# Loads, sums and transposes of the second and third batch put at other places, and the last output block in two parts, in a fused attention and mixer kernel

## The chip, the cores and the metric

The kernel runs on one core of a Trainium2 chip. The metric is the time of one execution on the device in microseconds, the median of several runs. A core has five engines that work side by side, each on its own list of instructions in order: TensorE (PE, matmuls; PEld is its weight load), VectorE (DVE), ScalarE (ACT), GpSimd (POOL) and SyncE (SP), which here only issues transfers. They meet through semaphores. Transfers (DMA) run beside them; those that SP issues show up as queue q1, those that GpSimd issues as q0, and ScalarE's as q10.

## The reference

Attention with normalized queries and keys, over 8 batches, 12 heads, 448 rows and 64 columns, and a mixer on the heads put side by side (448 x 768 for each batch):

```python
q_n = q / (norm(q) + 1e-6);  k_n = k / (norm(k) + 1e-6)
attn = softmax(q_n @ k_n.T / tau)
x = (attn @ v), heads side by side            # 448 x 768
u = x + (x.T @ U @ V).T                       # rank 32, over the rows
out = u + max(u @ w_ch1, 0) @ w_ch2           # 768 -> 3072 -> 768
```

## The kernel before

Heads are worked on in **pairs**, six in a batch, numbered 0 to 47 over all batches; `NP` is 6, so pairs 6 to 11 are batch 1 and 12 to 17 batch 2. Inputs come in **groups** of mostly two pairs: group 5 holds pairs 8 and 9, group 6 holds 10 and 11, group 7 holds 12 and 13, group 8 holds 14 and 15. A group's q, k and v are loaded by SP (`load`) into one of three staging buffers (`NST`), two transfers for q, four each for k and for v. Then the group is prepared (`Prep`): `square` of q and of k (mostly on GpSimd, L243), `reduce` to sums (VectorE, L248), `root` (ScalarE, L253 and L254), `invert` (VectorE, L260 and L262), `scale` (GpSimd, L268, four for a group), and `values`, the cast of v to bf16 (GpSimd, L276).

A pair's scaled q and k are transposed: up to pair 11 by eight matmuls on TensorE (L300) and a copy on VectorE (L305), from pair 12 on by a transposing transfer that SP issues (L315, name `T` in the schedule). Scores follow (L331, L324 and L343), their exponentials on ScalarE (L356, L353), the product with the values in two halves (L376, L383), each divided on VectorE (L394, then L395, which writes X). Both halves of a pair up to the tenth use the same PSUM bank. Then comes the low-rank part: `A` (L416, up to pair 10 with X as an operand), its copy on ScalarE (L422), X's transpose (L430) and `H` (L441) with its copy to u (L446). From pair 10 on these are done for two pairs at once, with X transposed by SP (L461), L469, L483 and the sums L488 into uE or uO, the two buffers of u. V, the rank-32 matrix, is needed for this in four copies, one on each 32 partitions: `load_copies` brings three more of them, `place_copies` casts them (L152 to L154).

The mixer of a batch is cut into small steps that fill TensorE between the attention steps of the next batch. `steps_m1` makes 24 blocks of six matmuls (L513, 448 columns) with a relu on ScalarE (L517) or VectorE (L519). `steps_m2` takes for each half of the 768 output columns three or four blocks of 128 rows, each 24 matmuls of 384 columns (L540) in four steps of six. Batch 0 adds u by three more matmuls (L550) and copies the block out on ScalarE (L554) or VectorE (L556); later batches add it on VectorE (L558). L564, L568 and L571 store the blocks. After the last pair, nothing but the last batch's mixer is left.

The order is written out by hand. Batch 0's attention has a list of words. From pair 6 on, a loop over `n` names a few places in each pair's turn (index 0, 1, ... of `order`), and between places puts as many mixer steps as `spread` gives. Preparations, loads and weight loads are hung on such places with `put(n, index, ...)`. A place fixes an instruction's turn in its engine's own list, and not a time: an engine that has nothing to wait for runs ahead. `Estimate` adds up rough costs for TensorE, ScalarE and VectorE while the program is written, and `act_first` picks from them the engine for a relu, or for batch 0's copy of a block:

```python
a = max(t["act"], t["pe"]) + act_us
d = max(t["dve"], t["pe"]) + dve_us
if a <= d: ...   # ScalarE, otherwise VectorE
```

The weights `w1_sb` and `w2_sb` are loaded on GpSimd's queue, w1 in four pieces and w2 in two halves of two pieces each: `load_w2(0, 0, 12)` and `load_w2(0, 12, 24)` for the first half of the columns. They are 32-bit in memory and arrive as bf16.

Of the kernel before, what the change touches and what calls it, by code (L numbers as in the profile page):

```python
# [9 lines left out]
FP = mybir.dt.float32  # L10
# [12 lines left out]
def kernel(  # L23
# [17 lines left out]
    nc = tc.nc  # L41

    B, H, S, D = q.shape
    C = H * D
    R = moe_U.shape[-1]
    F = moe_w_ch1.shape[-1]
    NP = H // 2
    CC = C // 128
    NC = F // 128
    HC = C // 2  # L50
# [3 lines left out]
    work = ctx.enter_context(tc.tile_pool(name="work", bufs=2))  # L54
# [30 lines left out]
    est = Estimate()  # L85
# [39 lines left out]
    V_raw = work.tile([128, S], FP, name="V_raw", tag="ut", bufs=2)  # L125
# [3 lines left out]
    w2_sb = const.tile([128, NC, C], BF, name="w2_sb")  # L129
# [29 lines left out]
    def load_copies():  # L159

        for r0 in (32, 64, 96):
            nc.gpsimd.dma_start(out=V_raw[r0:r0 + R, :], in_=moe_V)

    def place_copies():
        place_v(nc.gpsimd.tensor_copy, slice(0, 128))
# [5 lines left out]
    def load_w2(half, n0, n1):  # L171
        cols = slice(half * HC, (half + 1) * HC)
        nc.gpsimd.dma_start(
            out=w2_sb[:, n0:n1, cols],
            in_=moe_w_ch2[n0 * 128:n1 * 128, cols].rearrange("(n p) d -> p n d", p=128))


    groups = []
# [11 lines left out]
    def load(gi, what, *engs):  # L190
        b, p0, n = groups[gi]
        engs = list(engs) * 4
        h0, nh = 2 * p0, 2 * n
        s = gi % NST

        def src(x, hs, lo, hi, c):
            return x[b, hs, lo:hi, :].rearrange("h (p c) d -> p h (c d)", c=c)

        def dst(t, ps, hs, c):
            return t[ps, hs, 0:c, :].rearrange("p h c d -> p h (c d)")  # L200

        L, U2 = slice(0, 64), slice(64, 128)
        if what == "q":
            allh = slice(h0, h0 + nh)
            engs[0].dma_start(out=dst(qst[s], L, slice(0, nh), 4), in_=src(q, allh, 0, 256, 4))
            engs[1].dma_start(out=dst(qst[s], U2, slice(0, nh), 3), in_=src(q, allh, 256, 448, 3))
            return
        x, t = (k, kst[s]) if what == "k" else (v, vst[s])
        m = min(3, nh)
        ou, mi = slice(h0, h0 + nh, 3), slice(h0 + 1, h0 + m)  # L210
        engs[0].dma_start(out=dst(t, L, slice(0, nh, 3), 4), in_=src(x, ou, 0, 256, 4))
        engs[1].dma_start(out=dst(t, U2, slice(0, nh, 3), 3), in_=src(x, ou, 256, 448, 3))
        engs[2].dma_start(out=dst(t, L, slice(1, m), 3), in_=src(x, mi, 0, 192, 3))
        engs[3].dma_start(out=dst(t, U2, slice(1, m), 4), in_=src(x, mi, 192, 448, 4))
# [66 lines left out]
    def by_dma(n):  # L281

        return n >= 2 * NP
# [25 lines left out]
    def step_T(b, p):  # L309
        if not by_dma(b * NP + p):  # L310
            pe_T(b, p)
            evict_T(b, p)
            return
        gi, j = group_of[(b, p)]
        nc.sync.dma_start_transpose(  # L315
            out=new_qkT(b, p).rearrange("p a (c r) -> p (a c) r", r=128),
            in_=norm[gi][0][:, j, :, :, :, :].rearrange("p i c h d -> p (i c h d)"))
# [92 lines left out]
    def u_of(b):  # L410
        return uE if b % 2 == 0 else uO
# [82 lines left out]
    ut_of = {}  # L494
# [30 lines left out]
    def steps_m2(b):  # L525
        u = u_of(b)
        if b % 2 == 0:
            chunks = [(64 + 128 * c, 128 * c, c) for c in range(3)]
        else:
            chunks = [(384, 384, 3)] + [(128 * c, 128 * c, c) for c in range(3)]  # L530
        steps = []
        state = {}

        def part(half, ci, lo, hi):
            r0, u0, c = chunks[ci]
            if lo == 0:
                state["mp"] = psum.tile([128, HC], FP, name="mp", tag="ps_m", bufs=2)
            mp = state["mp"]
            for f in range(lo, hi):
                nc.tensor.matmul(out=mp, lhsT=relu[:, f, r0:r0 + 128],  # L540
                                 rhs=w2_sb[:, f, half * HC:(half + 1) * HC],
                                 start=(f == 0), stop=(b > 0 and f == NC - 1), skip_group_check=True)
            est.pe(0.97)
            if hi < NC:
                return
            o = work.tile([128, HC], FP, name="o_sb", tag="o_sb", bufs=3)
            if b == 0:
                for i in range(3):
                    cc = half * 3 + i
                    nc.tensor.matmul(out=mp[:, i * 128:(i + 1) * 128], lhsT=u[:, cc, u0:u0 + 128],  # L550
                                     rhs=ident, start=False, stop=(i == 2), skip_group_check=True)
                est.pe(0.17)
                if est.act_first(0.48, 0.55):
                    nc.scalar.copy(out=o, in_=mp)  # L554
                else:
                    nc.vector.tensor_copy(out=o, in_=mp)  # L556
            else:
                nc.vector.tensor_add(o.rearrange("p (k d) -> p k d", d=128),  # L558
                                     mp.rearrange("p (k d) -> p k d", d=128),
                                     ut_of[(b, half)][:, :, c, :])  # L560
                est.dve(0.55)
            cols = slice(half * HC, (half + 1) * HC)
            t4 = out[b, 0:256, cols].rearrange("(p c) d -> c p d", c=4)
            nc.sync.dma_start(out=t4[c], in_=o[0:64, :])  # L564
            if c < 3:
                t3 = out[b, 256:448, cols].rearrange("(p c) d -> c p d", c=3)
                other = nc.scalar if b == B - 1 and half == 1 else nc.sync
                other.dma_start(out=t3[c], in_=o[64:128, :])  # L568
            else:
                t4e = out[b - 1, 0:256, cols].rearrange("(p c) d -> c p d", c=4)  # L570
                nc.sync.dma_start(out=t4e[3], in_=o[64:128, :])  # L571

        for half in range(2):
            for ci in range(len(chunks)):
                for i in range(4):
                    steps.append(lambda half=half, ci=ci, i=i: part(half, ci, 6 * i, 6 * i + 6))
        return steps
# [8 lines left out]
    def f(n):  # L586
        for _ in range(n):
            fill.pop(0)()

    def load_all(gi):  # L590
        if gi < len(groups):
            for x in ("q", "k", "v"):
                load(gi, x, nc.sync)

    load(0, "k", nc.sync, nc.scalar)
    load(0, "q", nc.sync, nc.scalar)
# [10 lines left out]
    def T(n):  # L607
        step_T(*pairs[n])
# [124 lines left out]
    def put(n, at, fn):  # L733
        after.setdefault((n, at), []).append(fn)

    for gi in range(5, len(groups)):
        m, g = first_pair[gi], preps[gi]
        if m == NP + 2:
            at = [(NP, 1), (NP, 2), (NP + 1, 6), (NP, 5), (NP + 1, 0), (NP + 1, 1)]
            when = (NP + 1, 2)  # L740
        elif m == NP + 4:
            at = [(NP + 2, 0), (NP + 2, 1), (NP + 2, 6), (NP + 2, 4), (NP + 2, 6), (NP + 2, 7)]
            when = (NP + 3, 0)
        elif m == 2 * NP:
            at = [(m - 3, 6), (m - 3, 6), (m - 1, 0)] + [(m - 2, i) for i in (0, 1, 2)]
            when = (m - 2, 3)
        elif m == 2 * NP + 2:
            at = [(m - 2, i) for i in (0, 0, 5, 2, 3, 4)]
            when = (m - 2, 5)
        else:  # L750
            at = [(m - 3, 0), (m - 3, 0), (m - 3, 5)] + [(m - 2, i) for i in (0, 1, 2)]
            when = (m - 2, 3)

        put(*at[0], lambda g=g: g.square(0))
        put(*at[1], lambda g=g: g.square(1))
        put(*at[2], lambda g=g: g.values())
        put(*at[3], lambda g=g: g.reduce(0))
        put(*at[4], lambda g=g: g.reduce(1))
        put(*at[5], lambda g=g: g.root())
        put(*when, lambda g=g: (g.invert(), [g.scale(i, j, P_) for j in (0, 1) for i in (1, 0)]))  # L760
        if gi > 5 and m - 6 <= NP:
            put(*((NP, 3), (NP + 3, 0))[gi - 6], lambda gi=gi: load_all(gi))
        elif gi > 5:
            at = {2 * NP + 2: [(m - 4, 5), (m - 4, 6), (m - 3, 2)],
                  2 * NP + 4: [(m - 4, i) for i in (0, 2, 4)]}.get(m, [(m - 6, 4), (m - 5, 5), (m - 4, 3)])
            for x, w in zip("qkv", at):
                put(*w, lambda gi=gi, x=x: load(gi, x, nc.sync))
        if by_dma(m):
            put(m - 1, -1, lambda m=m: T(m))
            put(m - 1, 0, lambda m=m: T(m + 1))  # L770

    put(NP, 2, lambda: load_w1(2304, 3072))
    put(NP, 3, lambda: (load_w2(0, 0, 12), load_w2(0, 12, 24)))
    put(NP + 1, 2, lambda: (load_w2(1, 0, 12), load_w2(1, 12, 24)))
    put(NP + 3, 0, load_copies)
    put(NP + 5, 5, place_copies)

    def spread(n, order, nf, first=0):
# [14 lines left out]
    for n in range(NP, NPAIR + 1):  # L793
        b, p = pairs[n] if n < NPAIR else (B, 0)
# [116 lines left out]
```

## Time and profile before

| what | value |
|---|---|
| median of three runs | 581.62 us (581.51 to 582.03) |
| span of the profiled run | 580.3 us |
| TensorE busy | 568.6 us, 98% of the span |
| ScalarE, GpSimd, VectorE busy | 261.0, 215.1, 213.1 us |
| TensorE's clock granted | full speed throughout, but for the idle end |
| transfers | 74.52 MB, on average 128 GB/s |
| bytes on SP's queue and on GpSimd's | 63.03 MB and 10.18 MB |
| weight pieces on GpSimd's queue | 8, median 18.8 us from issue to landing |
| V's copies on GpSimd's queue | 56 KB each, median 17.4 us to landing |
| outputs on SP's queue | 96 KB each, median 2.2 us to landing |

A row of the stretches of busy time gives the stretch, its length, then each engine's busy time with the number of its instructions in brackets (TensorE, weight load, VectorE, ScalarE, GpSimd), the granted clock, the share of the sixteen DMA engines that was busy, and GB/s. A row of the waits reads: engine, tile and line that waited, what released it, microseconds in total, how many times, the longest. A row of the chain of waits gives start, length and what was done. A queue's row gives packets, MB and the time of its packets as a share of sixteen engines' time. Ends of matmuls are modelled, and a little later than the next matmul's start.

### The profile page before, as it was taken

The page shows a single profiled execution, that of the slowest core. Times are in us where ns is not written, and L with a number is a line of the kernel's source. Part 1 is how long each engine was busy: PE and PEld are TensorE (multiplying, and loading weights), DVE is VectorE, ACT ScalarE, POOL GpSimd, SP SyncE. Part 2 cuts the span into 40 slices and gives each one's busy share as a digit, 9 for nine tenths or more (in the row PEclk, how much of TensorE's full clock was granted, in tenths as well). Part 3 has the DMA queues.
Part 4 walks back from the last instruction along what each step waited for, and adds up shares of the span by engine and source line. Part 5 has one row for each costly group of instructions (what it writes and reads, how often), then busy time and mean ns, then how long its engine had stood idle before and what let it go on. Part 6 is the DMA issues. An engine that isn't in the chain of part 4 may idle for free.

```text
span 580.3 us, 12249 instructions
## 1 busy us (share of the span) xinstructions
PE 568.6 (98%) x5074; PEld 327.1 (56%) x5074; DVE 213.1 (37%) x461; ACT 261.0 (45%) x447; POOL 215.1 (37%) x205
## 2 busy tenths in 40 slices
PE   7999999999999999999999999999999999999997
PEld 6665565555565556555655555655555545655554
DVE  6874551433243334423324343432244332320011
ACT  5876544455333653446324455246443374214200
POOL 8754866515326236426055063253261420000000
PEclk9999999999999999999999999999999999999999
DMA  6999999767486375584465763783655640231022
GB/s 163 193 244 236 238 211 221 181 124 138 103 158 155 88 154 114 135 162 105 88 160 137 128 137 96 145 175 81 134 125 117 132 74 16 54 72 35 7 49 56
DMA packets 139673, 74.52 MB, mean 128 GB/s; under 512 B 86656, under 2 KB 139440, under 8 KB 139616
## 3 DMA queue, kind: packets, MB, share of 16 engines
q1 hardware_dynamic: 129344, 63.03, 50.0%
q0 software_dynamic: 9728, 10.18, 10.3%
q8 instruction: 40, 0.66, 0.4%
q10 hardware_dynamic: 544, 0.51, 0.3%
q14 instruction: 17, 0.14, 0.1%
HBM read 52.19 MB, written 11.01 MB: 109 GB/s over the span
## 4 chain that ended last, share of the span: by engine, by line
PE 87%; DMA 7%; DVE 2%; SPq 1%; ACT 1%; POOL 1%; issue 0%; DVEq 0%; POOLq 0%; ACTq 0%
PE mp L540 38%; PE mp L513 33%; DMA w_sb<-in_moe_w_ch_dram 5%; PE sc L331 5%; PE av L383 3%; PE up L383 2%; DMA kst<-in_k_dram 2%; PE av L343 1%; PE av L376 1%; PE up L376 1%; PE up L469 1%; DMA qst<-in_q_dram 1%; PE av L483 1%; DVE ss L248 1%; ACT E L356 0%
## 5 line engine op out<-in xcount | busy, mean ns | idle before, releaser
L540 PE MATMUL mp<-w_sb,relu 128*128 128x384 bf16 x1344 | 233.6, 327 | 0.8 <-DMA w_sb<-in_moe_w_ch_dram 0.8
L540 PEld LDWEIGHTS <-relu 128*128 128x128 bf16 x1344 | 125.2, 98 | 90.6 <-issue 14.0
L513 PEld LDWEIGHTS <-w_sb 128*128 128x128 bf16 x1128 | 105.0, 98 | 99.2 <-issue 9.3
L517 ACT ACTIVATE relu<-mp 128x448 bf16<-128x448 f32 x162 | 88.0, 543 | 128.4 <-PE mp L513 128.4
L356 ACT ACTIVATE E<-sc 128x896 bf16<-128x896 f32 x144 | 125.2, 923 | 23.6 <-PE sc L331 22.6
L268 POOL TENSOR_TENSOR qk<-kst,inv 128x512 bf16<-128x512 f32 x43 | 45.9, 1069 | 240.7 <-DVE inv L262 236.2
L513 PE MATMUL mp<-uO,w_sb 128*128 128x448 bf16 x576 | 114.3, 353 | 0.0
L513 PE MATMUL mp<-uE,w_sb 128*128 128x448 bf16 x552 | 112.9, 353 | 0.0
L558 DVE TENSOR_TENSOR o_sb<-mp,ut 128x384 f32<-128x384 f32 x50 | 27.8, 557 | 141.4 <-PE mp L540 140.1
L248 DVE TENSOR_REDUCE ss<-sq 128x16 f32<-128x1024 f32 (+1 forms) x50 | 57.8, 1165 | 1.0 <-ACT sq L240 1.0
L268 POOL TENSOR_TENSOR qk<-qst,inv 128x512 bf16<-128x512 f32 x44 | 47.3, 1077 | 1.6 <-PE up L441 1.6
L383 PEld LDWEIGHTS <-E 128*128 128x128 bf16 x1152 | 45.0, 97 | 0.0
L519 DVE TENSOR_SCALAR relu<-mp 128x448 bf16<-128x448 f32 x26 | 16.2, 625 | 78.0 <-PE mp L513 77.5
L331 PE MATMUL sc<-qkT 64*64 64x448 bf16 x576 | 42.4, 360 | 0.6 <-ACT E L356 0.3
L243 POOL TENSOR_TENSOR sq<-kst 128x1024 f32<-128x1024 f32 (+1 forms) x23 | 42.6, 1856 | 0.1
L243 POOL TENSOR_TENSOR sq<-qst 128x1024 f32<-128x1024 f32 x21 | 39.7, 1892 | 3.3 <-DMA qst<-in_q_dram 3.3
L353 ACT ACTIVATE E<-av 128x448 bf16<-128x448 f32 x17 | 9.2, 541 | 47.3 <-PE up L343 47.3
L276 POOL CAST v<-vst 128x1024 bf16<-128x1024 f32 (+1 forms) x25 | 25.0, 1003 | 9.9 <-DMA vst<-in_v_dram 7.7
L383 PE MATMUL av<-v,E 128*128 128x65 bf16 x624 | 28.0, 193 | 0.0
L473 ACT CAST A_sb<-up 128x128 bf16<-128x128 f32 x19 | 5.0, 263 | 47.6 <-PE up L469 47.6
L394 DVE RECIPROCAL rd<-av 128x4 f32<-128x4 f32 x52 | 9.3, 178 | 46.2 <-PE av L383 46.2
L376 PEld LDWEIGHTS <-E 128*128 128x128 bf16 x192 | 18.0, 98 | 14.6 <-issue 0.8
(98 smaller groups left out, 348.9 us busy)
## 6 DMA issues: line engine op xcount, KB each, us to landing
out_dram<-o_sb SPq DMA_DIRECT2D x109, 96.0 KB, 2.2
w_sb<-in_moe_w_ch_dram POOLq DMA_DIRECT2D x8, 1152.0 KB, 18.8
qst<-in_q_dram SPq DMA_DIRECT2D x23, 256.0 KB, 3.9
vst<-in_v_dram SPq DMA_DIRECT2D x46, 128.0 KB, 2.9
kst<-in_k_dram SPq DMA_DIRECT2D x44, 128.0 KB, 2.8
qst<-in_q_dram SPq DMA_DIRECT2D x23, 192.0 KB, 4.0
vst<-in_v_dram SPq DMA_DIRECT2D x46, 96.0 KB, 2.7
kst<-in_k_dram SPq DMA_DIRECT2D x44, 96.0 KB, 2.7
```

The lines of the kernel that those rows point to most:

```text
L243: nc.gpsimd.tensor_mul(sq[:, 0:self.nh * 4, :], self.flat(t), self.flat(t))
L248: nc.vector.reduce_sum(self.ss[:, j, 0:self.nh * 4], self.sq[j][:, 0:self.nh * 4, :], axis=AX.X)
L268: eng.tensor_mul(qks[self.gi % 2][:, j, i, :, :, :], t[:, 2 * j:2 * j + 2, :, :].rearrange("p h c d -> p c h d"), iv.unsqueeze(3).to_broad ...
L276: nc.gpsimd.tensor_copy(out=self.flat(v65[self.s])[:, :, 0:D], in_=self.flat(vst[self.s]))
L331: nc.tensor.matmul(out=sc[o:o + 64, h, 0:S], lhsT=t[r, 1, c * 128 + o:c * 128 + o + 64], rhs=t[r, 0, 0:S], start=True, stop=True)
L356: nc.scalar.activation(out=e[:, 2 * c:2 * c + 2, 0:S], in_=sc[:, :, 0:S], func=AF.Exp)
L376: nc.tensor.matmul(out=av[:, i, :, :], lhsT=last_of(b, p)[:, ic * 128:(ic + 1) * 128], rhs=vv[:, 2 * j:2 * j + 2, 3, :], start=(i == 0), s ...
L383: nc.tensor.matmul(out=av[:, i, h, :], lhsT=e[:, 2 * c + h, ic * 128:(ic + 1) * 128], rhs=vv[:, 2 * j + h, c, :], start=False, stop=(i == ...
L513: nc.tensor.matmul(out=mp, lhsT=w1_sb[:, cc, f * 128:(f + 1) * 128], rhs=u[:, cc, 0:S], start=(cc == 0), stop=(cc == CC - 1))
L517: nc.scalar.activation(out=relu[:, f, o:o + S], in_=mp, func=AF.Relu)
L540: nc.tensor.matmul(out=mp, lhsT=relu[:, f, r0:r0 + 128], rhs=w2_sb[:, f, half * HC:(half + 1) * HC], start=(f == 0), stop=(b > 0 and f == ...
L558: nc.vector.tensor_add(o.rearrange("p (k d) -> p k d", d=128), mp.rearrange("p (k d) -> p k d", d=128), ut_of[(b, half)][:, :, c, :])
```

## The change

It moves work of the second and third batch to other places, and splits the last output block:

- V's three copies are loaded on SP's queue instead of GpSimd's, and hung on pair 8 instead of pair 9.
- Group 5's sums, root and inverse take earlier places, in front of pair 7's turn. Group 7's second sum, root and inverse move ahead by one place each. Group 8's sums and root move back by one.
- Group 6's values are loaded at pair 8 instead of with q and k at pair 6, and cast at pair 10 instead of pair 8. Group 7's values are loaded at pair 10 instead of with q and k at pair 9. Group 8's q, k and v are asked for in pair 11's turn instead of pairs 10 and 11.
- The transposes of pair 12 are asked for at the end of pair 10's turn, in front of group 8's loads, and those of pair 13 just after.
- The very last block (24 matmuls of 384 columns) becomes one of 256 and one of 128 columns, each with its own add and its own stores, in steps of twelve matmuls. The number of steps stays four.
- The planner's cost for a step of L540 is worked out from its columns.

Its purpose is to have the sums and the weights ready when TensorE asks for them, and to leave less to do behind the last matmul.

```diff
     def load_copies():
         for r0 in (32, 64, 96):
-            nc.gpsimd.dma_start(out=V_raw[r0:r0 + R, :], in_=moe_V)
+            nc.sync.dma_start(out=V_raw[r0:r0 + R, :], in_=moe_V)
...
-        def part(half, ci, lo, hi):
+        def part(half, ci, lo, hi, c0=0, c1=HC):
...
-            mp = state["mp"]
+            mp = state["mp"][:, c0:c1]
             for f in range(lo, hi):
                 nc.tensor.matmul(out=mp, lhsT=relu[:, f, r0:r0 + 128],
-                                 rhs=w2_sb[:, f, half * HC:(half + 1) * HC],
+                                 rhs=w2_sb[:, f, half * HC + c0:half * HC + c1],
...
-            est.pe(0.97)
+            est.pe(0.0004 * (c1 - c0 + 6) * (hi - lo))
...
+                if (b, half, ci) == (B - 1, 1, len(chunks) - 1):
+                    for cs in ((0, 256), (256, 384)):
+                        for i in range(2):
+                            steps.append(lambda half=half, ci=ci, i=i, cs=cs:
+                                         part(half, ci, 12 * i, 12 * i + 12, *cs))
+                    continue
...
         if m == NP + 2:
-            at = [(NP, 1), (NP, 2), (NP + 1, 6), (NP, 5), (NP + 1, 0), (NP + 1, 1)]
-            when = (NP + 1, 2)
+            at = [(NP, 1), (NP, 2), (NP + 1, 6), (NP, 3), (NP, 5), (NP, 6)]
+            when = (NP + 1, 0)
         elif m == NP + 4:
-            at = [(NP + 2, 0), (NP + 2, 1), (NP + 2, 6), (NP + 2, 4), (NP + 2, 6), (NP + 2, 7)]
+            at = [(NP + 2, 0), (NP + 2, 1), (NP + 4, 0), (NP + 2, 4), (NP + 2, 6), (NP + 2, 7)]
             when = (NP + 3, 0)
         elif m == 2 * NP:
-            at = [(m - 3, 6), (m - 3, 6), (m - 1, 0)] + [(m - 2, i) for i in (0, 1, 2)]
-            when = (m - 2, 3)
+            at = [(m - 3, 6), (m - 3, 6), (m - 1, 0), (m - 3, 6)] + [(m - 2, i) for i in (0, 1)]
+            when = (m - 2, 2)
         elif m == 2 * NP + 2:
-            at = [(m - 2, i) for i in (0, 0, 5, 2, 3, 4)]
+            at = [(m - 2, i) for i in (0, 0, 5, 3, 4, 5)]
             when = (m - 2, 5)
...
         if gi > 5 and m - 6 <= NP:
-            put(*((NP, 3), (NP + 3, 0))[gi - 6], lambda gi=gi: load_all(gi))
+            at = (((NP, 3), (NP, 3), (NP + 2, 0)), ((NP + 3, 0), (NP + 3, 0), (NP + 4, 4)))[gi - 6]
+            for x, w in zip("qkv", at):
+                put(*w, lambda gi=gi, x=x: load(gi, x, nc.sync))
         elif gi > 5:
-            at = {2 * NP + 2: [(m - 4, 5), (m - 4, 6), (m - 3, 2)],
+            at = {2 * NP + 2: [(m - 3, i) for i in (0, 1, 3)],
...
         if by_dma(m):
-            put(m - 1, -1, lambda m=m: T(m))
-            put(m - 1, 0, lambda m=m: T(m + 1))
+            first = m == 2 * NP
+            put(*((m - 2, 6) if first else (m - 1, -1)), lambda m=m: T(m))
+            put(m - 1, -1 if first else 0, lambda m=m: T(m + 1))
...
-    put(NP + 3, 0, load_copies)
+    put(NP + 2, 2, load_copies)
```

In `at` the six entries are the places of square(q), square(k), values, reduce(q), reduce(k) and root; `when` is that of invert and the four scales; `m` is the group's first pair.

More of the change, by code (lines that the diff above doesn't have):

```diff
@@ L537, in part @@
                 state["mp"] = psum.tile([128, HC], FP, name="mp", tag="ps_m", bufs=2)
-            mp = state["mp"]
+            mp = state["mp"][:, c0:c1]
             for f in range(lo, hi):
                 nc.tensor.matmul(out=mp, lhsT=relu[:, f, r0:r0 + 128],
-                                 rhs=w2_sb[:, f, half * HC:(half + 1) * HC],
+                                 rhs=w2_sb[:, f, half * HC + c0:half * HC + c1],
                                  start=(f == 0), stop=(b > 0 and f == NC - 1), skip_group_check=True)
-            est.pe(0.97)
+            est.pe(0.0004 * (c1 - c0 + 6) * (hi - lo))
             if hi < NC:
                 return
-            o = work.tile([128, HC], FP, name="o_sb", tag="o_sb", bufs=3)
+            o = work.tile([128, HC], FP, name="o_sb", tag="o_sb", bufs=3)[:, c0:c1]
             if b == 0:
@@ L559, in part @@
                                      mp.rearrange("p (k d) -> p k d", d=128),
-                                     ut_of[(b, half)][:, :, c, :])
+                                     ut_of[(b, half)][:, c0 // 128:c1 // 128, c, :])
                 est.dve(0.55)
-            cols = slice(half * HC, (half + 1) * HC)
+            cols = slice(half * HC + c0, half * HC + c1)
             t4 = out[b, 0:256, cols].rearrange("(p c) d -> c p d", c=4)
@@ L588, in f @@
             fill.pop(0)()
[L590 to L593, printed above, removed]
     load(0, "k", nc.sync, nc.scalar)
```

## The prediction

> **What bounds the kernel now.** I read the page first, then busy time by stretches, then TensorE's waits, the chain of waits from 57 to 90 us, and the queues there.
>
> ```profile
> PE 568.6 (98%) x5074; PEld 327.1 (56%) x5074; DVE 213.1 (37%) x461; ACT 261.0 (45%) x447; POOL 215.1 (37%) x205
> ```
> ```profile
> 92.00:112.00 20.00, 20.00 (x197) 12.06 (x195) 7.80 (x16) 9.16 (x15) 8.91 (x10) 1.00 0.87 186
> 112.00:545.00 433.00, 433.00 (x3725) 242.34 (x3724) 143.24 (x310) 193.48 (x334) 142.15 (x114) 1.00 0.54 114
> 576.20:580.30 4.10, 0.00 (x0) 0.00 (x0) 0.56 (x1) 0.00 (x0) 0.00 (x0) 0.78 0.18 48
> ```
> TensorE (first figure after the comma) has no idle time from 92 to 576 us. Nothing that moves other engines' work there can gain; it can only lose. What can be won lies before 92 us and behind the last matmul. TensorE's waits name three places past 45 us:
> ```profile
> PE mp L540 <- DMA w_sb<-in_moe_w_ch_dram: 0.8, 1, 0.8
> PE av L416 <- DVE X L395: 0.5, 1, 0.5
> PE tp L300 <- POOL qk L268: 0.5, 1, 0.5
> ```
> Modelled matmul ends hide part of each, so I take starts from TensorE's timeline. Eight transposes and what follows lie 0.45 us apart: 56 ns each. Six L540 matmuls take 0.98 us.
> - Pair 8's transposes: the first four start at 59.52, the others at 60.36, not 59.74: **0.62 us lost**.
> - L540 behind four L430 at 79.28 could start at 79.49; it starts at 80.46: **0.97 us lost**.
> - L416 behind six L540 at 85.97 could start at 86.95; it starts at 87.60: **0.65 us lost**.
>
> Together 2.24 us. The chain shows what stands before the last two:
> ```profile
> 50.89 29.52 DMA w_sb<-in_moe_w_ch_dram
> 80.46 1.14 PE mp L540 x6
> ...
> 81.82 0.62 DVE uO L446
> 82.44 1.13 DVE ss L248
> ...
> 83.57 0.56 DVE o_sb L556
> ...
> 84.71 1.14 DVE ss L248
> ...
> 85.87 0.33 ACT ss L253
> ...
> 86.70 0.35 DVE inv L262
> ...
> 87.12 0.43 DVE X L395
> ...
> 87.60 0.38 PE av L416 x4
> ```
> The first wait is for the second piece of `load_w2(0, ...)`, 29.5 us under way. Then VectorE runs without a break from L446 to X: 5.8 us of work against the 5.52 us that TensorE needs from L441 (81.43) to L416. Traffic by queue, from 62 to 74 us, then from 78 to 86 us:
> ```profile
> q0 software_dynamic: 1896, 1.45, 76.7%
> q1 hardware_dynamic: 1737, 1.40, 46.0%
> ```
> ```profile
> q0 software_dynamic: 2132, 1.61, 130.5%
> ```
> The weights (q0) move at 1.45 MB / 12 us = 121 GB/s beside SP's loads (q1), and at 1.61 / 8 = 201 GB/s alone.
>
> **What the Trainium skill says.** "DMA: Bandwidth & Descriptors", section Queues, rings and completion order: each DMA engine takes turns between the queues that have work, a packet at a time. The trace agrees: 1896 to 1737 packets. Same page, section Issuing engines are not separate DMA queues: another issuing engine saves only the issue time. So V's copies cost the weights their share from SP as well; what goes is 1.56 us of issuing on GpSimd (77.30). Same page, section Anatomy of one DMA: most of a small transfer's time is a fixed completion of about 2 us; here a 96 KB output lands in 2.2 us. "TensorE: Matmul & The Clock Gate", section Back-to-back issue gap: N/2.4 + 2.5 ns for one matmul, but about 81 ns at N=128 in a stream of weight load and matmul. The trace gives 163 ns at 384 columns (162.5 by the formula) and 56 ns at 128 columns with a new weight each.
>
> **The change part by part.**
>
> *Group 5 sooner (pairs 8, 9).* reduce(1), root and invert move ahead of pair 7. reduce(1) now runs at 55.07, behind two L519, though its squares were done at 49.07; it can follow reduce(0), from 51.0 to 52.2. The root then follows the exponentials that end at 53.8 on ScalarE, 0.6 us; invert is done at about 55.2, not 58.08. GpSimd's scales (58.23 on) start some 2.9 us sooner, and the second, which ends at 60.31, ends near 57.4, before TensorE asks at 59.5. The relus at 53.39 and 54.53 lie behind the moved reduce. Gain: 0.62 us, to 78.87 at the weight wait.
>
> *Loads.* On SP nothing stands between group 6's keys and values, so "later" doesn't move those values: still 50.75 to 58. V's three copies follow (three times 56 KB), then group 7's q and k. Group 7's v (448 KB, issued 65.74 to 70.30) goes behind the first output, at 84. So before 80 us q1 carries 448 - 172 = 276 KB less. At q1's 1.40 MB / 12 us = 117 GB/s that is 2.4 us in which q0 gets 80 GB/s more, 189 KB, or 0.94 us of its rate alone. The second piece lands near 79.45, not 80.4. I take it; the bounds are 0.4 (V's 1792-byte rows cost as much as the values did) and 1.59 (all of 0.97 + 0.62). Since TensorE comes at 78.87, it waits some 0.6 us, and this place with the one before gives **1.0 us**.
> What queues behind the moved loads: values(7) on GpSimd at 91.25 needs its v, issued near 85 to 88 and some 3 to 5 us under way; behind it stand V's casts (95.83) and group 8's squares (96.94), whose sums were at 103.22. Slack of some 4 us.
>
> *Group 7's sums.* reduce(0) stays right behind L446; reduce(1) comes before the o_sb copy and the first divide instead of after. The work on VectorE is the same, so the order alone gains nothing: X would still end 6.1 us behind L441. But the planner decides the copy's engine. By its costs ScalarE ends at 0.25 + 2 x 0.93 + 0.48 = 2.59 us from pair 10's start, VectorE at 0.62 + 1.235 + 0.55 = 2.41, so the copy went to VectorE (L556). With reduce(1) in front VectorE stands at 3.64 and ScalarE takes it, behind its exponentials (82.15 to 83.88), which costs nothing there. That cuts 0.5 us from VectorE: X ends some 5.7 us behind L441 against 5.52 needed. **0.4 us** of the 0.65 go; bounds 0 and 0.65. New wait: pair 9's second half needs the bank that the first divide frees, now behind both sums: 3.9 us behind L441, against 4.05 when TensorE asks. It just fits.
>
> *Transposes of pair 12, group 8's loads.* T(12) stood behind eight issues at 92.90; now it goes when the scales allow, near 88. T(12) and T(13) take 4.35 us of SP; q and k of group 8 go behind them, to about 94 to 98 instead of 85 to 89. Pair 12's scores are at 98.83, so nobody waited and nothing is won; it protects against TensorE coming sooner. Group 8's squares slip from 96.94 to about 98 to 102, ahead of their sums. SP then reaches pair 11's transpose of X about when it did (105.38), while TensorE wants it 1.4 us sooner: landed by some 107.8, wanted at 108. Cost nothing, with little to spare; the uO copy behind it has 0.9 us before L513 starts at 112.41.
>
> *Last block in two.* 24 matmuls of 256 and 24 of 128 columns: 24 x (109 + 56 - 163) ns = 0.05 us more; with 81 ns for the short ones 0.65 us more. The last add shrinks from 0.56 us (384 columns) to about 0.29, by the line through 448: 0.62 and 256: 0.42. The last transfer is 32 KB instead of 96; its completion stays, perhaps 0.2 us go. The first part's outputs leave 1.3 us sooner and lie beside the second's matmuls. Net **0.4 us**, bounds -0.35 and 0.5. `est.pe` now counts 0.936 us for six matmuls, not 0.97; a relu may change engines, which is free while TensorE has no wait.
>
> Sum: 1.0 + 0.4 + 0.4 = 1.8 us; 581.62 - 1.8 = **579.8 us**.
>
> **The rivals.**
> - *No change to measure, 581.2.* The weights land as before, so the 0.62 won at pair 8 is waited off at 80.46, and VectorE's chain keeps its length; only the tail gives 0.4. For it: V's copies come in the room of the values, and group 6's values don't move. Against: 276 KB less at 117 GB/s.
> - *More, 578.9.* Both waits and the 0.65 us vanish and the tail gives 0.5: 1.59 + 0.65 + 0.5 = 2.74. For it: GpSimd is free 2.9 us sooner, 1.56 us of issuing is gone. Against: both rest on bytes and on VectorE's order, and neither sum reaches that far.
> - *Slower, 583.3.* Pair 11's transpose or group 8's sums come late in SP's new order, and L513 at 112.41 stalls for some 2 us beyond its slack; the short matmuls cost 81 ns, leaving the tail 0.35 us worse; the early gain is 0.6: 581.62 + 2 + 0.35 - 0.6 = 583.4, say 583.3. For it: no slack to speak of at 108 us, eight SP issues moved. Against: everything past 92 us now runs with no gap.
>
> **How the numbers follow.** Forecast 0.56, more 0.18, no change 0.18, slower 0.08. The first two are over 0.2% (1.16 us) faster; the forecast with its low bounds (0.4 + 0 + 0.3 us) would not be, and is counted in the third: faster 0.74, same 0.18, slower 0.08. The range takes the second rival whole and reaches to the first: 578.8 to 581.2. Outside lie the slower case and the edges of the others.
>
> **What would show it.** Right: pair 8's eight transposes without a break; a wait for w_sb of 0.3 to 0.7 us, ending near 79.5; that copy on ScalarE; L416's wait at about 0.2; one L558 add of 128 columns near 0.29 us; 92 us to the end about as long as now less 0.4. Wrong: the weight wait still ending past 80.2, a new wait between 92 and 115 us, most likely for XT, uO or qkT, or short matmuls 80 ns apart.

## The result, and the profile after

| | before | after |
|---|---|---|
| median of the runs taken side by side | 582.0 us | 579.8 us |
| lowest to highest | 581.51 to 583.17 (6 runs) | 579.24 to 581.94 (6 runs) |
| span of the profiled run | 580.3 us | 577.7 us |

The ratio is 0.9963 with a 95% interval of 0.9945 to 0.9982, that is 2.2 us less, between 1.0 and 3.2. The first experiment runs the same kernel again, beside the kernel before, and gives 579.96 us and a ratio of 0.9969 (0.9957 to 0.9981).

The page's row of busy times, after:

```profile
PE 568.7 (98%) x5098; PEld 329.3 (57%) x5098; DVE 211.8 (37%) x460; ACT 261.9 (45%) x449; POOL 213.8 (37%) x202
```

TensorE has 24 matmuls more, for the last block in two parts, and is busy for as long as before. So the time came out of its idle time. Busy time by stretches of the changed kernel (start and end, length, TensorE, weight load, VectorE, ScalarE, GpSimd, clock, DMA share, GB/s):

```profile
45.00:60.00 15.00, 15.00 (x136) 8.09 (x134) 6.01 (x11) 10.54 (x19) 11.34 (x10) 1.00 1.14 234
60.00:76.00 16.00, 16.00 (x164) 9.17 (x162) 8.65 (x17) 9.64 (x18) 9.27 (x9) 1.00 1.25 232
76.00:80.50 4.50, 4.50 (x50) 2.83 (x46) 1.56 (x4) 0.81 (x3) 4.50 (x4) 1.00 1.31 203
80.50:92.00 11.50, 11.50 (x134) 7.48 (x127) 5.30 (x12) 7.28 (x12) 5.04 (x5) 1.00 1.30 216
112.00:545.00 433.00, 433.00 (x3724) 242.63 (x3722) 143.27 (x310) 193.06 (x334) 139.96 (x112) 1.00 0.54 114
```

From 45 to 92 us, where TensorE had been idle at three places, it now has no idle time. The long stretch behind is as it was: from pair 12's first scores to the last block's first matmul it is 473.29 us in both kernels (98.83 to 572.12, then 96.60 to 569.89). The three places on TensorE's timeline (start, length, what ran, how many; where there is idle time, it stands with its releaser at the end of a row):

```profile
59.55 0.61 PE L300 MATMUL tp<-ident,qk 128*128 128x128 bf16 x8
...
78.68 0.36 PE L430 MATMUL up<-ident,X 128*128 128x128 bf16 x4
78.87 1.14 PE L540 MATMUL mp<-w_sb,relu 128*128 128x384 bf16 x6
79.85 0.35 PE L441 MATMUL up<-V_sb,A_sb 128*128 128x448 bf16 x1
...
84.39 1.14 PE L540 MATMUL mp<-w_sb,relu 128*128 128x384 bf16 x6
85.36 0.39 PE L416 MATMUL av<-X,U_sb 128*128 128x128 bf16 x4
```

Pair 8's eight transposes are one row, without a break. L540 follows L430 with no wait, and L416 follows the six L540 after 0.97 us, which is what they take. Up to the first L540 that uses the second weight piece, 80.46 - 78.87 = 1.59 us are won, at L416 0.65 more, in the last block 0.37 (8.17 us from its first matmul to the span's end before, 7.80 after). The sum, 2.61 us, is the difference of the spans, 2.6.

The repeat of this kernel shows one thing differently. Its chain of waits from 76 us on begins so:

```profile
50.85 28.48 DMA w_sb<-in_moe_w_ch_dram
79.33 0.04 issue
79.38 1.14 PE mp L540 x6
80.51 0.19 PE up L441
```

Here the weights landed at 79.33, close to the 79.45 of the prediction, and TensorE did wait. In the first profile they were issued half a microsecond sooner (50.37) and landed at 78.59, before TensorE asked at 78.8. The two spans of one kernel, 577.7 and 578.2, differ by as much as the two starts of L540 do. Of its 2.1 us of span, this run has 1.08 up to that L540, of which 0.16 is an earlier arrival at pair 8 (59.36 instead of 59.52), then 0.65 and 0.37.

### The profile page after: what moved, and what is told of

It is laid out like the page before. It is cut to its first block, busy times and chain, and to the rows that moved or that the text cites. A ratio compares the mean times of both kernels' runs of the same rounds, so it can differ in the third digit from the quotient of the medians.

```text
span 577.7 us, 12301 instructions
## 1 busy us (share of the span) xinstructions
PE 568.7 (98%) x5098; PEld 329.3 (57%) x5098; DVE 211.8 (37%) x460; ACT 261.9 (45%) x449; POOL 213.8 (37%) x202
## 4 chain that ended last, share of the span: by engine, by line
PE 95%; DVE 1%; ACT 1%; SPq 1%; DMA 1%; issue 0%; DVEq 0%; ACTq 0%
PE mp L540 39%; PE mp L513 37%; PE sc L331 6%; PE av L383 3%; PE up L383 2%; PE av L376 1%; PE av L343 1%; PE tp L300 1%; PE sc L655 1%; PE up L376 1%; PE up L469 1%; DMA qst<-in_q_dram 1%; PE av L483 1%; ACT E L356 0%; PE sc L324 0%
## 5 line engine op out<-in xcount | busy, mean ns | idle before, releaser
L540 PE MATMUL mp<-w_sb,relu 128*128 128x384 bf16 (+2 forms) x1368 | 233.7, 323 | 0.0
L540 PEld LDWEIGHTS <-relu 128*128 128x128 bf16 x1368 | 126.7, 98 | 88.4 <-issue 13.1
L513 PEld LDWEIGHTS <-w_sb 128*128 128x128 bf16 x1128 | 105.1, 98 | 99.1 <-issue 9.7
L513 PE MATMUL mp<-uO,w_sb 128*128 128x448 bf16 x576 | 114.2, 352 | 0.0
L513 PE MATMUL mp<-uE,w_sb 128*128 128x448 bf16 x552 | 112.9, 353 | 0.0
L558 DVE TENSOR_TENSOR o_sb<-mp,ut 128x384 f32<-128x384 f32 (+2 forms) x51 | 28.0, 549 | 141.0 <-PE mp L540 141.0
L383 PEld LDWEIGHTS <-E 128*128 128x128 bf16 x1152 | 45.0, 97 | 0.0
L383 PE MATMUL av<-v,E 128*128 128x65 bf16 x624 | 28.0, 193 | 0.0
L376 PEld LDWEIGHTS <-E 128*128 128x128 bf16 x192 | 18.0, 98 | 14.5 <-issue 0.8
```

The lines of the kernel that those rows point to most:

```text
L376: nc.tensor.matmul(out=av[:, i, :, :], lhsT=last_of(b, p)[:, ic * 128:(ic + 1) * 128], rhs=vv[:, 2 * j:2 * j + 2, 3, :], start=(i == 0), s ...
L383: nc.tensor.matmul(out=av[:, i, h, :], lhsT=e[:, 2 * c + h, ic * 128:(ic + 1) * 128], rhs=vv[:, 2 * j + h, c, :], start=False, stop=(i == ...
L513: nc.tensor.matmul(out=mp, lhsT=w1_sb[:, cc, f * 128:(f + 1) * 128], rhs=u[:, cc, 0:S], start=(cc == 0), stop=(cc == CC - 1))
L540: nc.tensor.matmul(out=mp, lhsT=relu[:, f, r0:r0 + 128], rhs=w2_sb[:, f, half * HC + c0:half * HC + c1], start=(f == 0), stop=(b > 0 and f ...
```

## The experiments

All edits are made to the changed kernel, unless another is named. "Lost" is TensorE's time by starts, as the prediction counts it.

**The changed kernel again**, with no edit.

> The changed kernel once more, as the measure for the others of this set. Theory (three waits removed and a shorter tail): ratio to before about 0.996; TensorE without a wait from 45 us to the last matmul, the last add 0.29 us. Rival (one lucky profile): one of the three waits shows again, most likely the one for w_sb near 79 us, since in the first profile the second piece landed near 78.7 us and TensorE asked at 78.87 us.

Measured: 579.96 us, ratio 0.9969 (0.9957 to 0.9981), span 578.2. The row of L540 ends in the wait that the first profile did not have:

```profile
78.48 0.36 PE L430 MATMUL up<-ident,X 128*128 128x128 bf16 x4
79.38 1.14 PE L540 MATMUL mp<-w_sb,relu 128*128 128x384 bf16 x6 [0.53 <-DMA w_sb<-in_moe_w_ch_dram]
```

0.69 us are lost by starts. Four kernels below leave everything up to this place as the change has it, which makes six profiles of one order. In them the weights landed at 78.35, 78.59, 78.72, 78.85, 79.05 and 79.33, and TensorE lost 0, 0, 0.12, 0.19, 0.10 and 0.69 us. So the repeat is the extreme, and in most runs little or nothing is lost here.

**Group 5's sums at their old places.**

```diff
-            at = [(NP, 1), (NP, 2), (NP + 1, 6), (NP, 3), (NP, 5), (NP, 6)]
-            when = (NP + 1, 0)
+            at = [(NP, 1), (NP, 2), (NP + 1, 6), (NP, 5), (NP + 1, 0), (NP + 1, 1)]
+            when = (NP + 1, 2)
```

> Group 5's sums, root and inverse back at their old places, all else as changed. Theory: pair 8's eight transposes break in the middle again by about 0.6 us, the weights are there by then, so nothing is given back: about 0.6 us over the changed kernel (ratio to before near 0.997). Rival (the weights are what TensorE meets last, so what is lost at pair 8 is hidden in that wait): same time as the changed kernel.

Measured: 579.88 us, ratio 0.9969 (0.9958 to 0.9981), span 578.1. TensorE's timeline has the break back, and no wait for the weights (they landed at 79.02):

```profile
59.33 0.39 PE L300 MATMUL tp<-ident,qk 128*128 128x128 bf16 x4
60.18 0.40 PE L300 MATMUL tp<-ident,qk 128*128 128x128 bf16 x4 [0.46 <-POOL qk L268]
...
79.09 0.36 PE L430 MATMUL up<-ident,X 128*128 128x128 bf16 x4
79.29 1.14 PE L540 MATMUL mp<-w_sb,relu 128*128 128x384 bf16 x6
```

L540 starts at 79.29 here, at 79.38 in the repeat above and at 78.87 in the first profile. What the sooner sums win at 60 us is waited off at 79 us when the weights land at 79.3; it counts in full only when they land by 78.8. By the other landings above it should be worth some 0.4 us or more in most runs (an estimate); the medians don't show it.

**Group 7's values sooner again**, with its q and k.

```diff
-            at = (((NP, 3), (NP, 3), (NP + 2, 0)), ((NP + 3, 0), (NP + 3, 0), (NP + 4, 4)))[gi - 6]
+            at = (((NP, 3), (NP, 3), (NP + 2, 0)), ((NP + 3, 0), (NP + 3, 0), (NP + 3, 0)))[gi - 6]
```

> Group 7's values asked for with its q and k again, as before the change; V's copies stay on SP. Theory (bytes beside the weights): 448 KB at 117 GB/s are 3.8 us in which the weights lose 80 GB/s, so their second piece lands about 1.5 us later, near 80.2 us, and TensorE waits for w_sb by some 1.2 us: 1.2 us over the changed kernel. Rival (what helped was GpSimd issuing its weight loads sooner and being rid of V's copies): no wait for w_sb, same time as the changed kernel.

Measured: 581.73 us, ratio 1.0003 (0.9992 to 1.0014), span 579.0.

```profile
80.14 1.14 PE L540 MATMUL mp<-w_sb,relu 128*128 128x384 bf16 x6 [1.28 <-DMA w_sb<-in_moe_w_ch_dram]
```

The weights landed at 80.09, later than in any of the six profiles above, and 1.44 us were lost. So the later load of these values does bring the weights sooner. The queues from 74 to 78 us (packets, MB, share of the time of sixteen engines), in this kernel, then in the changed one:

```profile
q0 software_dynamic: 687, 0.53, 84.0%
q1 hardware_dynamic: 527, 0.41, 40.9%
```
```profile
q0 software_dynamic: 1074, 0.81, 131.3%
q1 hardware_dynamic: 7, 0.01, 0.6%
```

In these 4 us SP's queue takes 0.41 MB in one case and 0.01 in the other, and the weights get 0.28 MB less or more. The median is 1.8 us above the repeat's. The wait in the profile explains 0.75 us of it against the repeat and 1.3 against the first profile; the profiled run (580.73 us) was one of this kernel's faster ones, and what the others lost was not seen.

**Group 7's sums, root and inverse at their old places.** The first sum stays right behind L446 in both orders; the second moves.

```diff
-            at = [(m - 3, 6), (m - 3, 6), (m - 1, 0), (m - 3, 6)] + [(m - 2, i) for i in (0, 1)]
-            when = (m - 2, 2)
+            at = [(m - 3, 6), (m - 3, 6), (m - 1, 0)] + [(m - 2, i) for i in (0, 1, 2)]
+            when = (m - 2, 3)
```

> Group 7's second sum, root and inverse at their old places, by which the planner gives the first block's copy to VectorE again (L556) instead of ScalarE (L554). Theory: VectorE's run from L446 to X takes 6.1 us again and L416 waits about 0.6 us: 0.6 us over the changed kernel. Rival (L416's wait came from TensorE arriving at a bad moment behind the weight wait, and is gone with that): no wait at L416, same time.

Measured: 580.46 us, ratio 0.9977 (0.9967 to 0.9987), span 578.2.

```profile
85.92 0.38 PE L416 MATMUL av<-X,U_sb 128*128 128x128 bf16 x4 [0.49 <-DVE X L395]
```

The 0.65 us are lost again, and the median is 0.5 to 0.7 us above those of the changed kernel, though the intervals overlap. Which part of the edit wins them, the order on VectorE or the copy's engine, the next two tell apart.

**The order alone: batch 0's first copy kept on VectorE.**

```diff
-                if est.act_first(0.48, 0.55):
+                if (False if (half, ci) == (0, 0) else est.act_first(0.48, 0.55)):
```

> The changed kernel with the first block's copy of batch 0 forced back to VectorE, the sums where the change put them. Theory (the engine of the copy is what counts, the order of the sums is not): VectorE has the same work between L446 and X as before, L416 waits 0.6 to 0.75 us, 0.5 to 0.6 us over the changed kernel (about 580.5). Rival (the order counts): L416 waits less than 0.2 us and the time is that of the changed kernel.

Measured: 580.39 us, ratio 0.9972 (0.9961 to 0.9983), span 578.1. VectorE's timeline, from the sums to X:

```profile
80.79 2.33 DVE L248 TENSOR_REDUCE ss<-sq 128x16 f32<-128x1024 f32 x2
83.05 0.55 DVE L556 COPY o_sb<-mp 128x384 f32<-128x384 f32 x1
83.51 0.17 DVE L394 RECIPROCAL rd<-av 128x4 f32<-128x4 f32 x1
...
85.28 0.42 DVE L395 TENSOR_TENSOR X<-av,rd 128x256 bf16<-128x256 f32 x1
```

X ends at 85.70, which is 5.84 us behind L441's start; it was 6.11 in the kernel before. L416 comes only 0.08 us late, but pair 9's second half (L376) waits 0.29 us for the bank that the first divide frees. Together 0.37 us are lost instead of 0.65. About half of what the order alone wins is a wait for ScalarE. In the kernel before, the root (L254) ends at 86.45 and L260 starts at 86.48, 0.73 us behind the copy L305; in this run, with the second sum done sooner, L260 follows L305 after 0.59 us.

**The copy alone: the kernel before, with that copy on ScalarE.**

```diff
-                if est.act_first(0.48, 0.55):
+                if (True if (half, ci) == (0, 0) else est.act_first(0.48, 0.55)):
```

> The kernel before with nothing changed but that copy, forced to ScalarE. Theory: VectorE's run from L446 to X is 0.5 us shorter, L416's wait falls from 0.65 to about 0.15 us, the other two waits stay: 0.5 us under the kernel before (ratio about 0.999). Rival (order of the sums): wait and time as before.

Measured: 582.07 us, ratio to the kernel before 1.0005 (0.9996 to 1.0014), span 580.1. VectorE's timeline:

```profile
82.17 1.21 DVE L248 TENSOR_REDUCE ss<-sq 128x16 f32<-128x1024 f32 x1
83.87 0.18 DVE L394 RECIPROCAL rd<-av 128x4 f32<-128x4 f32 x1 [0.50 <-PE av L383]
...
84.43 1.21 DVE L248 TENSOR_REDUCE ss<-sq 128x16 f32<-128x1024 f32 x1
```

Where the copy was, VectorE now idles for 0.50 us: the divide needs the product of pair 9's first half (L383), which is not ready. X ends 6.12 us behind L441, as before, and L416 waits as before. In that order the copy cost nothing on VectorE.

**The transposes of pair 12 and group 8's loads at their old places.**

```diff
-            at = {2 * NP + 2: [(m - 3, i) for i in (0, 1, 3)],
+            at = {2 * NP + 2: [(m - 4, 5), (m - 4, 6), (m - 3, 2)],
...
-            first = m == 2 * NP
+            first = False
```

> The transposes of pairs 12 and 13 and group 8's loads at their old places, all else as changed. Theory (the move only protects, and is now needed): SP issues pair 12's transposes behind group 8's q and k, near 92 us, and they land 2 to 4 us later, near 94 to 96; pair 12's first scores are asked for at 96.6: a wait at L331 for qkT of 0 to 1 us, time 0 to 1 us over the changed kernel. Rival (needless): no wait for qkT at all and the same time; also XT lands no later.

Measured: 581.15 us, ratio 0.9988 (0.9975 to 1.0002), span 578.7.

```profile
97.62 0.57 PE L331 MATMUL sc<-qkT 64*64 64x448 bf16 x8 [0.73 <-DMA qkT<-qk]
```

The transposes are issued at 94.19, and the scores start 2.84 us behind the first of the twelve L540 ahead of them instead of 2.05, which is 0.79 us late. The edit is needed once TensorE arrives sooner; that it would have won nothing in the kernel before is argued from its profile, which has no wait there, and was not run. The median lies 1.2 us above the repeat's, again more than the wait in the profile.

**The last block whole.**

```diff
-                    for cs in ((0, 256), (256, 384)):
-                        for i in range(2):
+                    for cs in ((0, 384),):
+                        for i in range(4):
...
-                                         part(half, ci, 12 * i, 12 * i + 12, *cs))
+                                         part(half, ci, 6 * i, 6 * i + 6, *cs))
```

> The last block whole again, all else as changed. Theory: the last add takes 0.56 us again and the last transfer is 96 KB; from the last matmul's end to the end of the span 4.1 us instead of about 3.7; TensorE saves 0.05 us; 0.35 to 0.4 us over the changed kernel. Rival (the short matmuls eat it, 81 ns each): the last block's 48 matmuls take 0.6 us more than 24 whole ones, and the time without the split is lower or the same.

Measured: 580.29 us, ratio 0.9968 (0.9956 to 0.9980), span 577.9. VectorE's last rows, in this kernel, then in the changed one:

```profile
573.88 0.56 DVE L558 TENSOR_TENSOR o_sb<-mp,ut 128x384 f32<-128x384 f32 x1 [3.34 <-PE mp L540]
```
```profile
572.71 0.43 DVE L558 TENSOR_TENSOR o_sb<-mp,ut 128x256 f32<-128x256 f32 x1 [2.06 <-PE mp L540]
574.05 0.29 DVE L558 TENSOR_TENSOR o_sb<-mp,ut 128x128 f32<-128x128 f32 x1 [0.91 <-PE mp L540]
```

From its first matmul to the span's end the block takes 8.16 us whole and 7.80 split: 0.36 us by the profile, though the times, with overlapping intervals, can't show so little.

The 0.37 us against the kernel before are a sum of four terms. The last add is 0.27 us shorter, and the last matmuls take 0.06 us more. ScalarE's part of the last output lands 2.03 us after its issue instead of 2.37, so 0.34 are won. But from that landing to the end of the span it now takes 1.28 us, not 1.10. What lies there is the close of the program: SP goes through eight waits, 0.06 us apart and always in the same order, one for each of eight semaphores that the transfers of SP and ScalarE use in turn. The waits that are left once the last output has landed (line, engine, how many, their nanoseconds, first and last start), before, after, and in the next experiment's kernel:

```profile
L906 SPq EVENT_SEMAPHORE  x4: 28/28/28, 579.2 to 579.4; - x4
```
```profile
L911 SPq EVENT_SEMAPHORE  x7: 28/28/28, 576.4 to 576.8; - x7
```
```profile
L911 SPq EVENT_SEMAPHORE  x2: 28/28/28, 576.4 to 576.5; - x2
```

SP and ScalarE issue 446, 451 and 448 transfers in these three kernels, and this number decides on which of the eight semaphores the last one falls.

**V's copies back on GpSimd's queue and at pair 9**, the only edit.

```diff
-            nc.sync.dma_start(out=V_raw[r0:r0 + R, :], in_=moe_V)
+            nc.gpsimd.dma_start(out=V_raw[r0:r0 + R, :], in_=moe_V)
...
-    put(NP + 2, 2, load_copies)
+    put(NP + 3, 0, load_copies)
```

> V's three copies back on GpSimd's queue and at pair 9, all else as changed. Theory (bytes beside the weights): 172 KB fewer on SP's queue before 80 us bring the weights' second piece some 0.6 us sooner, so no wait for w_sb; GpSimd issues for 1.6 us in front of group 7's squares, which end near 82.1 instead of 80.5 us, about when VectorE's second sum wants them (82.0): the changed kernel's time or up to 0.5 us less. Rival (getting them off GpSimd was part of the gain): the squares come late, L416 waits 0.3 us or more, and it is slower than the changed kernel.

Measured: 579.16 us (578.93 to 579.25), ratio 0.9950 (0.9937 to 0.9964), span 577.4. The weights landed at 78.44 and TensorE did not wait. The 1.56 us of issuing on GpSimd are back (76.64), its squares of group 7 end at 81.97, and L416 comes 0.08 us late. **The same kernel again**, since it has the lowest median of all:

> The version with V's copies on GpSimd's queue at pair 9 once more. Theory (172 KB fewer beside the weights leave 0.3 to 0.6 us of slack at the weight place): no wait for w_sb, ratio to before again near 0.995, its interval below or about the changed kernel's 0.9969. Rival (a lucky set of runs): a w_sb wait of 0.3 us or more, ratio back at 0.9965 to 0.997.

Measured: 579.19 us (578.93 to 580.14), ratio 0.9941 (0.9922 to 0.9961), span 577.7, again with no wait for the weights (landed at 78.56). Two medians that agree lie 0.6 to 0.8 us below the two of the changed kernel. The intervals overlap in part. Of this, 0.30 us have nothing to do with the weights: with three transfers fewer on SP's queue only two closing waits are left behind the last landing, and the last block takes 7.50 us to the span's end in both profiles. It takes 7.80 in all nine profiles that have the split block and V's copies on SP's queue.

**V's copies on SP's queue, but behind group 7's values.**

```diff
-    put(NP + 2, 2, load_copies)
+    put(NP + 4, 5, load_copies)
```

> V's three copies on SP, but behind group 7's values at pair 10, all else as changed. Theory: the weights come 0.6 us sooner as in the run before; but SP has 1.8 us more to issue ahead of pair 12's transposes and of XT of pair 11, which landed 0.5 us too late for VectorE already: L488 waits up to 2 us for XT, and L513 on uO near 110 us begins to wait, 0 to 1 us. Net between 0.5 us faster and 0.5 us slower than the changed kernel. Rival (SP has room to spare there): no wait at L513, 0.5 us faster.

Measured: 579.89 us, ratio 0.9962 (0.9950 to 0.9975), span 578.1. The weights landed at 78.30, but TensorE came to them only at 79.3 without having waited for them: this run was already 0.43 us behind the first profile at pair 8's transposes (59.98 against 59.55). The row for uO shows a wait of 1.17 us for X's transpose, against 0.50 in the first profile and 1.12 in the repeat; it delayed no matmul. For the weights this run does not tell the place of these loads from their queue. For the end it does: the last block takes 7.80 us, so the 0.30 us go with the queue.

**The weights asked for sooner.**

```diff
-    put(NP, 2, lambda: load_w1(2304, 3072))
-    put(NP, 3, lambda: (load_w2(0, 0, 12), load_w2(0, 12, 24)))
+    put(NP, 0, lambda: load_w1(2304, 3072))
+    put(NP, 0, lambda: (load_w2(0, 0, 12), load_w2(0, 12, 24)))
```

> GpSimd issues w1's last piece and w2's first two pieces in front of group 5's squares (index 0 of pair 6 instead of 2 and 3), all else as changed. Theory (the second piece of w2 is what TensorE meets last): the pieces are issued 2 to 4 us sooner, the weights' queue doesn't run dry between them, w_sb is there before 78.7 us in every run: no wait from 45 us on, median 0.3 to 0.6 us under the changed kernel and less spread. Rival (the squares, 1 to 3 us later, hold up pair 8's transposes; or SP's loads, with a smaller share, come late): a break of pair 8's transposes of 0.3 us or more, no gain.

Measured: 579.69 us (579.58 to 579.76), ratio 0.9960 (0.9947 to 0.9972), span 577.9. The second piece is issued at 44.63, 5.7 us sooner than in the first profile of the changed kernel, and lands at 79.08, not sooner. L540 is 0.15 us late. In this run asking sooner gained nothing; fewer bytes on the other queue did, as group 7's values show.

## Why the prediction was right, and where it was not

The forecast of 579.8 us and its range held. That the median is 579.8 to the digit is luck: 1.8 us less than 581.62 was forecast, and 2.2 us less than 582.0 was measured. By its own steps:

- **Group 5 and the weights: 1.0 us forecast, 0.90 to 1.59 measured by starts.** Invert was done at 54.90 (forecast 55.2), and the second scale ended at 57.12 (57.4). The landing of 79.45 came out as 79.33 in the repeat, but by 78.35 to 79.05 in the five other profiles of this order, and there 1.40 us or more were won. So the step was sized too small in most runs. It worked out the landing by a rate and had no room for a spread of 1.0 us between runs. (Its 276 KB take 448 KB of 1024 bytes and 172 of 1000; in one unit they are 280, which moves the landing by less than 0.05 us.) That one gain can be waited off in the other is shown by the run without the sooner sums against the repeat: L540 starts at 79.29 and 79.38.
- **The loads.** Group 6's values did not move (50.06 to 56.93). Group 7's did, and putting them back gives the weight wait back. V's copies were to cost the weights their share from SP's queue as well as from GpSimd's, and nothing was to be won by changing the queue. With both queue and place put back, the kernel is faster by some 0.7 us in two runs out of two. The prediction had no term for the larger part that can be named: 0.30 us at the close of the program, by the count of transfers on SP's and ScalarE's queues. The rest may be the weights, which landed at 78.30 to 78.56 in the three profiles without V's copies before them and at 78.35 to 79.33 in the six with them; these ranges overlap, so this part is argued and not shown.
- **Group 7: 0.4 us forecast, 0.65 measured, and the reason was wrong.** The step that failed is "the order alone gains nothing". VectorE's work was added up as if it ran without a break in any order. The prediction's own chain of waits shows otherwise: it leaves VectorE at 85.87 for ScalarE's root and comes back at 86.70. And in the old order VectorE's first divide waits for pair 9's first half in any case; the copy ahead of it lay in that wait. Taking it away alone gives 0 (X 6.12 us behind L441), the new order alone 0.28 of the 0.65, both together all of it (X 5.38 us behind L441, against 5.52 needed). The sum moved forward fills the time of the wait, and only then is the copy's time worth something; and it gets the root out of the way. That the planner would give the copy to ScalarE was right, and so was that it is free there: it ran at 82.17, straight behind the exponentials.
- **The new wait for the bank** was judged to "just fit", and does in the changed kernel; with the copy on VectorE it lasts 0.29 us.
- **Transposes and group 8's loads**: nothing won, a loss of 0.79 us prevented. The tight place that the prediction named showed up as a wait of VectorE alone. VectorE's timeline in the changed kernel:

```profile
108.30 0.62 DVE L488 TENSOR_TENSOR uO<-up,XT 128x448 bf16<-128x448 f32 x1 [0.50 <-DMA XT<-X]
108.84 0.38 DVE L491 COPY uO<-uE 128x384 bf16<-128x384 bf16 x1
```

  L513 starts at 110.18 without a wait. It needs the second L488, done at 108.92, which leaves 1.26 us; in the repeat 0.64 were left. The prediction counted the copy L491 as well, but L491 writes columns 448 to 511 of uO, and L513 reads columns 0 to 447: in the repeat L513 began at 110.69, before the copy's end at 110.73.
- **The tail: 0.4 us forecast, 0.37 measured, in part by luck.** The 128-column add takes 0.29 us as worked out, and the short matmuls follow each other 56 ns apart, not 81. But the smaller last transfer won 0.34 us, not 0.2, and the closing waits, which the prediction left out, took 0.18 back. The Trainium skill, "DMA: Bandwidth & Descriptors", section Anatomy of one DMA, states its fixed 2 us for transfers that GpSimd issues; the last two here are SP's and ScalarE's, and took 2.1 and 2.4 us with 96 KB, 1.8 and 2.0 with 32.

The rivals: of "no change", the part in which pair 8's gain is waited off at the weights came true in the repeat. "More" has its two waits gone in the first profile, whose gain of 2.61 us of span is close to its 2.74; the gains in the medians, 2.2 us and 2.0 in the repeat, lie between the two. For "slower", L513 was not delayed, and the short matmuls did not cost more.

What stays open: why the kernels with group 7's values sooner, and with the transposes at their old places, lose more in the median than their profiles show; why the run without the sooner sums is not slower in the median; and whether V's copies cost the weights anything by their place.

## What to carry to other kernels

Before you credit an engine with work taken off it, look at what the next instruction in its list waits for: work that lies in the shadow of such a wait is free, and gains come from putting other needed work into that shadow. Two gains in a row on one engine don't add up where the second place waits for a transfer; the landing of the transfer sets the sum. Here it came sooner by asking for fewer other bytes before it, not by asking for it sooner. An edit that removes no wait today may be what keeps the others' gain. When a small gain remains unexplained, look at the end of the program too: moving a transfer to another queue can change what is left to wait for there.

## What the runs showed of the hardware

- A weight piece asked for 5.7 us sooner (44.63 instead of 50.37) landed at 79.08 against 78.59 and 79.33. With group 7's 448 KB of values asked for on SP's queue ahead of it, it landed at 80.09.
- The same copy of 128 x 384 bf16 from uE to uO (L491) took 0.96 us in the kernel before, 0.38 in the changed one and 0.25 with V's copies on GpSimd's queue. Its length follows GpSimd's scale that is under way when it starts. In the kernel before, then in the changed one:

```profile
110.28 1.06 POOL L268 TENSOR_TENSOR qk<-qst,inv 128x512 bf16<-128x512 f32 x1
110.49 0.96 DVE L491 COPY uO<-uE 128x384 bf16<-128x384 bf16 x1
```
```profile
108.05 1.06 POOL L268 TENSOR_TENSOR qk<-qst,inv 128x512 bf16<-128x512 f32 x1
108.84 0.38 DVE L491 COPY uO<-uE 128x384 bf16<-128x384 bf16 x1
```

  In twelve of the fourteen profiles the copy ended 0.11 to 0.12 us behind the end of that scale. In the other two only 0.07 us of the scale were left, and the copy took 0.25 us, as it does in the changed kernel at 514.56 with GpSimd idle. No experiment moved the scale, so this is read from the traces alone.
- A last output of 96 KB on ScalarE's queue landed 2.37 us after its issue, one of 32 KB 2.03.
